# Causal mask by a selection after the exponential, 32-column merges with a copied block, two-step norms, row-wise transfers and a new step order in a delta-rule attention and mixture kernel

## The chip, the cores and the metric

One core of a Trainium2 chip runs the whole problem as one program. The metric is the device time of one execution in microseconds. Three runs of the kernel before gave 469.35, 471.07 and 987.01 us; the median, 471.07 us, is what a new time is compared with. The profile was taken on one more execution, which took 472.51 us.

## The reference, cut to what matters

Two layers follow each other. The first is a recurrence with a state per head (4 batches, 8 heads, 768 positions, head size 48); the second is a causal attention per expert (4 experts of width 64), whose two best experts per token are mixed with softmax weights.

```python
k_n = k / (np.linalg.norm(k, axis=-1, keepdims=True) + 1e-06)
for t in range(S):                       # state starts at zero
    y[:, :, t] = q[:, :, t] @ state
    v_old = state^T k_n[t]
    state = state + beta[t] * outer(k_n[t], v[t] - v_old)
x = y as (batch, 768, 384)
logits = x @ w_gate                      # the two largest of 4 are kept: w
for e in range(4):
    q, k, v = x @ wq[e], x @ wk[e], x @ wv[e]
    scores = 0.125 * q @ k^T
    scores = np.where(causal, -1e9, scores)
    a = softmax(scores)
    out += w[e] * (a @ v @ wo[e])
```

The lines above are shortened; `causal` is true above the diagonal.

## The kernel before, in words

**Tiling.** The recurrence is cut into chunks of 64 positions. Four chunks of all heads of two batches make a *unit*; there are 6 units (`n` = 0 to 5; 3 after each other for batches 0 and 1, 3 for batches 2 and 3), each with 4 chunks (`c`). The attention of a unit's 256 query positions goes by batch (`b`), pair of experts (`y`), and pairs of 128-key blocks (`kp`). A unit `n` has `s = n % 3` earlier units before it, so its scores run over `kp` = 0 to `s`; the pair with `kp == s` holds the diagonal.

**Within a chunk** the recurrence becomes a triangular system. `gram` (L219) multiplies the keys with themselves on TensorE. `st_in` (L255) turns the Gram blocks on VectorE so that each partition holds one 32x32 system. `solve_pre` (L267, steps 0 to 5) takes the diagonal, makes the norm of each key from a bit trick and three Newton steps for the square root (L277 to L279), the factor `aa` = beta / norm² (L285), its negative `nn` (L290, L293), and multiplies the system by it (L291 for unit 0 on VectorE, L294 for the other units on POOL). `solve_step` (L304, steps 1 to 32) eliminates: two TENSOR_TENSOR per step (L316 and L317), on POOL for units 1 to 5 and on VectorE (L319, L320) for unit 0; step 31 is an affine selection (L323), step 32 a product with `aa` (L329) and a copy (L330). `st_out` (L336) and `st_nat` (L332) turn the result back into `TG` (tile `tt`) and `TN` (tile `tn`). For units 1 to 5 `merge1` (L365) and `merge2` (L375) combine the two 32-halves of a chunk into a 64x64 inverse: `merge1` makes `-M` with products of 32 columns; `merge2` multiplies `TN` with two 32-column blocks at once, an identity that stands at index 0 of `lanes(n)` and the block of `merge1`, so that one 64-column product gives both the copied block and the new one, and ScalarE copies all 64 columns (L385). `clear` (L387) sets the block below to zero on POOL. Unit 0 is built in another way (`gram_up` L237, `diag` L339, `expand` L349): its Gram blocks are masked on VectorE (L244), 16-wide systems are solved, and products on TensorE expand them.

**The chain of states.** For each chunk: `ks`, `u`, `s`, `q`, `y` (L416 to L463) on TensorE with one ScalarE or VectorE step after each. Each chunk needs the state of the one before. `spread` (L464) moves rows of the output (`h3`, tile `h`) to other partitions of `xh` by six small transfers from SP's queue (L469), three for one half and then three for the other.

**The second layer.** `proj_qk` (L476) and `proj_v` (L501) accumulate nine products each: three pairs of high and low parts, and within each pair the three 128-row groups `r`. `max_list` (L544) forms scores with a mask added by two bf16 products (`identb`, `mbias`) per block and half, and takes maxima (L568). `score` (L598) forms the transposed scores from three products and a fourth that subtracts the maximum (`SEL`, `MR`), and for the diagonal pair adds the mask by two more bf16 products per block and half; ScalarE takes the exponential (L622, L624, L625) into `at`. `av` (L627) multiplies `at` with the values; `norm`, `fin_t`, `fin_o` finish and store.

**Matmul records.** All matmuls are issued by the helper `mm` (L115 and L116), so the profile shows them on L116 and they are told apart by their tiles (`pm__66` to `pm__69` are four rotating PSUM banks). A product with plain fp32 operands leaves two records, one with float32r operands or bf16 leaves one.

**The order.** Nothing is scheduled by a compiler: each engine's queue is in program order, and that order is the string `ORDER` (L36), a list of steps written out by hand or by a planner, which L728 runs one after the other. `sv3.7` is solve step 7 of unit 3; `+13` stands for 13 *filler* products of a zero tile (`zb`, 128x128 by 256, bf16, L125). 298 of these stand in the list, nearly all before the merges of unit 1 (`m1`, `m2`); one more is issued ahead of it. Step names: `gr` gram, `gu` gram_up, `gq` gram_q, `si` st_in, `so` st_out, `sn` st_nat, `m1`, `m2` the merges (`m13.0` is `merge1` of unit 3), `cl` clear, `vt` scale_v, `hx` spread, `pj`, `pv` the projections, `mx`, `mp`, `mr` the maxima, `sc` score, `nm` norm, `ft`, `fo` the end, `cb` small_consts, `kc` pick_rows, `w` weights, `lc`, `lg`, `lq` loads, `vs` ones, `gt` gates.

Of the kernel before, what the change touches and what calls it, by code (L numbers as in the profile page):

```python
# [21 lines left out]
ATB = 7  # L22
NP = 8
NT = CH * NP
# [12 lines left out]
+21 gr0.0 gr0.3 cb gr0.1 gr0.2 si0 gq0.1 pre0.0 gu2 w2 pre0.1 w3 pre0.2 pre0.3 pre0.4 pre0.5 +16 gu3 sv0.1 sv0.2 sv0.3  # L37
+4 gu1 sv0.4 w4 sv0.5 sv0.6 +34 gq0.3 sv0.7 sv0.8 sv0.9 lc0.1 vt0.1 sv0.10 sv0.11 sv0.12 lq1.1 sv0.13 sv0.14 +10 gu0
vt0.0 w0 sv0.16 +13 gq0.0 so0 +34 gr1.3 +6 gr1.2 w5 +10 gr1.1 gr1.0 sn0 dg1 dg0 lq1.2 kc0 si1 pre1.0 dg2 +27 ex1.0 +7
ex1.1 pre1.1 pre1.2 kc1 pre1.3 dg3 pre1.4 w1 kc3 w6 ex0.0 pre1.5 sv1.1 +12 ex2.0 sv1.2 sv1.3 sv1.4 ks0.0 gq0.2 ex0.1  # L40
ex1.2 +15 ex2.1 +2 ex0.2 ex3.0 sv1.5 sv1.6 sv1.7 sv1.8 +5 ex0.3 sv1.9 lq1.0 +7 u0.0 gq1.1 +1 s0.0 +5 ks0.1 y0.0 ex3.1
+7 ex3.2 lc0.2 ex1.3 sv1.10 q0.1 vs0 sv1.11 +3 u0.1 +5 s0.1 sv1.12 sv1.13 lc0.3 ex2.2 +7 ex2.3 vt0.2 ks0.2 ex3.3 kc2
lq1.3 y0.1 u0.2 sv1.14 sv1.15 vt0.3 sv1.16 sv1.17 sv1.18 lg2.1 +9 q0.2 s0.2 +6 ks0.3 hx0.1.0 lg2.3 y0.2 sv1.19 lg2.2
pj0.0.0 pj0.0.2 lg2.0 gq1.3 sv1.20 q0.3 u0.3 gr2.0 sv1.21 sv1.22 sv1.23 sv1.24 +1 y0.3 gq1.2 sv1.25 sv1.26 mx0.0.0.0
+9 mx0.1.0.0 lc1.0 sv1.27 vs1 sv1.28 pv0.0.0 hx0.3.0 gr2.1 s0.3 gq1.0 +1 pj0.1.2 q1.0 gr2.2 sv1.29 sv1.30 sv1.31
sv1.32 so1 vt1.0 ks1.0 lg3.0 sn1 gr2.3 pj0.1.0 pv0.1.1 si2 lq2.2 m11.0 m11.1 +2 m21.0 +2 m21.3 cl1 mx0.0.1.1 u1.0
pre2.0 m21.1 mp0.0 m21.2 s1.0 lc1.1 pre2.1 pre2.2 pv0.0.1 vt1.1 mr0.0 lc1.2 ks1.1 pre2.3 vt1.2 y1.0 pre2.4 vs2
sc0.0.1.0 pre2.5 sv2.1 mx0.1.1.1 u1.1 q1.1 +1 s1.1 pv0.1.0 ks1.2 sv2.2 lq2.1 lc1.3 sv2.3 vt1.3 sv2.4 mp0.1 y1.1 u1.2
sv2.5 sv2.6 mr0.1 sv2.7 sv2.8 sv2.9 sc0.0.0.0 lg3.1 sc0.1.0.0 sv2.10 gt0 lq2.0 q1.2 sv2.11 sv2.12 hx1.1.0 sv2.13
sv2.14 s1.2 av0.0.3 av0.0.1 av0.0.0 av0.0.2 sc0.1.1.0 lc2.0 vt2.0 ks1.3 lg3.3 y1.2 sv2.15 sv2.16 nm0.0 pj1.0.0 q1.3  # L50
u1.3 gq2.0 gr3.0 sv2.17 sv2.18 y1.3 sv2.19 ft0.0 pj1.0.2 gr3.3 s1.3 av0.1.0 sv2.20 mx1.0.0.0 av0.1.1 av0.1.2 av0.1.3
mx1.0.0.1 gq2.2 hx1.3.0 sv2.21 pj1.1.2 pj1.1.0 pv1.1.0 lq3.1 sv2.22 mx1.0.1.2 +1 mx1.0.1.3 pv1.0.0 gr3.1 ks2.0 mp1.0
sv2.23 lq3.0 lg3.2 gr3.2 sv2.24 gq3.0 sv2.25 sv2.26 sv2.27 mr1.0 sv2.28 fo0.0.1 sc1.0.0.0 sc1.0.1.1 q2.0 sv2.29 lg4.0
# [36 lines left out]
def tile_kernel(ctx, tc, kq, kv, beta, wqk, wvg, wo, consts, out):  # L90
# [34 lines left out]
    def filler():  # L125
        mm(PY0[:, 0, 256:512], ZB[:, 0:128], ZB, False)
# [62 lines left out]
    for x in DB:  # L189
        G.memset(x, 0.0)  # L190
# [608 lines left out]
```

## Time and profile before

| What | us |
|---|---|
| Median of three runs | 471.07 |
| The profiled execution itself | 472.51 |
| Its span, first to last instruction | 470.7 |
| PE busy in the span | 445.1 |
| VectorE / ScalarE / POOL busy | 283.6 / 210.0 / 229.4 |
| Fillers, 299 products, busy | 42.5 |

In the profile PE is the matmul side of TensorE and PEld its weight loads. Matmuls are pipelined: the duration of one record (some 0.2 us for a small one) says little about the pace, which is read from the starts of successive records in the timeline. The granted clock of TensorE was 0.967 of full speed on average.

### The profile page before, as it was taken

Reading aid. Unit: us, or ns where it says so; the run is one execution under the profiler, and the core shown is the slowest. Engines: PE = TensorE matmul, PEld = TensorE weight load, DVE = VectorE, ACT = ScalarE, POOL = GpSimd, SP = SyncE. Lnnn points to the kernel's source line nnn. Section 1 sums busy time; section 2 is a strip of 40 time slices with the busy share of each in tenths; the row PEclk is TensorE's granted clock in tenths of the full one; section 3 lists DMA queues with packets and bytes.
Section 4 is the critical chain, followed back from the end, with each engine's and each line's share of the span. In section 5 each row is a group of like instructions: output and inputs, shape, how many; then the busy total and the mean of one; then the engine's idle time right before and its main releaser. Section 6 shows DMA issues by size and latency. Waiting matters only on the chain.

```text
span 470.7 us, 24388 instructions
## 1 busy us (share of the span) xinstructions
PE 445.1 (95%) x11019; PEld 396.6 (84%) x11019; DVE 283.6 (60%) x636; ACT 210.0 (45%) x535; POOL 229.4 (49%) x392
## 2 busy tenths in 40 slices
PE   6898999899998999979999999999999999999997
PEld 4676887779887988878978998998999888888996
DVE  1799743249866495766976939556474745654312
ACT  2207411126554257334464464554555454635562
POOL 4314669852389847898078855589821010000000
PEclk9699999899999899988997999999999999999999
DMA  8610012302241221251131402013310110110002
GB/s 267 250 52 31 3 38 88 113 21 81 85 131 21 70 97 54 63 162 22 72 88 42 138 13 89 3 51 123 111 47 10 53 49 25 37 67 19 3 18 85
DMA packets 18967, 32.89 MB, mean 70 GB/s; under 512 B 2864, under 2 KB 8880, under 8 KB 18864
## 3 DMA queue, kind: packets, MB, share of 16 engines
q1 hardware_dynamic: 18864, 31.34, 21.1%
q8 instruction: 86, 1.41, 1.3%
q14 instruction: 17, 0.14, 0.1%
HBM read 24.25 MB, written 4.72 MB: 62 GB/s over the span
## 4 chain that ended last, share of the span: by engine, by line
PE 77%; DVE 7%; DMA 5%; SPq 4%; issue 3%; ACT 3%; POOL 1%; ACTq 0%; DVEq 0%
PE pm__67 L116 17%; PE pm__69 L116 15%; PE pm__68 L116 14%; PE pm__66 L116 14%; PE py L116 9%; PE xu L116 7%; SPq L469 4%; DMA xh<-h 3%; DMA qf<-in_kq_dram 2%; DMA kf<-in_kq_dram 1%; DVE B L320 1%; DVE tm L319 1%; ACT tt L232 1%; DVE rr L278 1%; ACT VS L347 1%
## 5 line engine op out<-in xcount | busy, mean ns | idle before, releaser
L317 POOL TENSOR_TENSOR B<-B,tm 128x30 f32<-128x30 f32 (+9 forms) x150 | 78.2, 521 | 11.8
L316 POOL TENSOR_TENSOR tm<-B 128x30 f32<-128x30 f32 (+9 forms) x150 | 75.2, 501 | 10.6
L148 POOL TENSOR_TENSOR kv<-kv,nt 128x384 f32<-128x384 f32 x24 | 19.9, 831 | 50.4 <-DMA kv<-in_kv_dram 38.4
L116 PE MATMUL py<-zb 128*128 128x256 bf16 x299 | 42.5, 292 | 1.3 <-DVE zb L121 1.1
L116 PEld LDWEIGHTS <-zb 128*128 128x128 bf16 x299 | 28.9, 104 | 8.0 <-DVE zb L121 1.1
L389 POOL MEMSET tt<- 32x1024 f32 x10 | 9.5, 946 | 34.9 <-PE pm__66 L116 13.2
L116 PE MATMUL py<-qf,sb 48*48 48x64 f32 x704 | 23.9, 218 | 1.0 <-DVE h L463 1.0
L116 PEld LDWEIGHTS py<-qf,sb 48*48 48x48 f32 x704 | 21.0, 120 | 3.2 <-DVE h L463 1.2
L568 DVE TENSOR_REDUCE mx<-pm__66 128x1 f32<-128x512 f32 (+3 forms) x28 | 18.1, 646 | 7.0 <-PE pm__67 L116 6.9
L429 ACT ACTIVATE ub<-xu 128x384 f32<-128x384 f32 x24 | 11.8, 493 | 22.0 <-PE xu L116 18.5
L462 DVE TENSOR_TENSOR xh<-py,xh 112x384 fp32r<-112x384 f32 x24 | 13.3, 556 | 13.0 <-ACT h L461 13.0
L460 ACT ACTIVATE xh<-py 112x384 fp32r<-112x384 f32 x24 | 11.8, 493 | 20.8 <-PE py L116 20.5
L260 DVE STREAM_TRANSPOSE B<-tt 32x1024 f32<-32x1024 f32 x10 | 19.8, 1978 | 0.2
L116 PE MATMUL xu<-xs,tt 64*64 64x48 f32 x768 | 17.9, 227 | 1.7 <-issue 1.4
L116 PE MATMUL pm__66<-xh,wqkh 128*128 128x256 f32 x96 | 16.9, 311 | 2.5 <-DMA xh<-h 2.3
L423 DVE TENSOR_TENSOR xs<-kv,xu 128x384 f32<-128x384 f32 x22 | 12.1, 548 | 11.7 <-PE xu L116 3.7
L568 DVE TENSOR_REDUCE mx<-pm__69 128x1 f32<-128x512 f32 (+3 forms) x24 | 14.9, 620 | 5.8 <-PE pm__66 L116 5.7
L116 PE MATMUL pm__69<-mbias,identb 64*128 64x128 bf16 x128 | 18.3, 225 | 0.0
L116 PEld LDWEIGHTS xu<-xs,tt 64*64 64x64 f32 x768 | 15.0, 142 | 3.8 <-issue 2.3
L116 PEld LDWEIGHTS pm__66<-xh,wqkh 128*128 128x128 f32 x96 | 14.4, 213 | 3.3 <-issue 2.8
L568 DVE TENSOR_REDUCE mx<-pm__67 128x1 f32<-128x512 f32 (+3 forms) x24 | 14.8, 616 | 2.9 <-PE pm__68 L116 2.9
L116 PE MATMUL pm__66<-mbias,identb 64*128 64x128 bf16 x114 | 16.4, 225 | 0.0
(358 smaller groups left out, 1610.4 us busy)
## 6 DMA issues: line engine op xcount, KB each, us to landing
kv<-in_kv_dram SPq DMA_DIRECT2D x24, 384.0 KB, 3.5
kf<-in_kq_dram SPq DMA_DIRECT2D x24, 256.0 KB, 3.7
qf<-in_kq_dram SPq DMA_DIRECT2D x24, 256.0 KB, 4.4
out_dram<-ot SPq DMA_DIRECT2D x24, 192.0 KB, 1.9
xh<-h SPq DMA_DIRECT2D x72, 32.0 KB, 2.1
wst<-in_wqk_dram SPq DMA_DIRECT2D x3, 256.0 KB, 5.5
csb<-in_consts_dram SPq DMA_DIRECT2D x1, 256.0 KB, 5.6
wst<-in_wvg_dram SPq DMA_DIRECT2D x1, 256.0 KB, 5.2
```

Of the source, the lines that this page charges most:

```text
L116: T.matmul(o, lhsT=a, rhs=b, start=start, stop=stop, skip_group_check=True)
L148: G.tensor_tensor(vt, vt, PR[n]["nt"][:, c * NP:c * NP + NP, None].to_broadcast([128, NP, HD]), op=OP.mult)
L260: V.transpose(B[r:r + 32], gf[r:r + 32, :, 0:32].rearrange("p t j -> p j t"))
L316: e.tensor_tensor(tv, bc(Z[:, i:i + 1, i + 1:]), bc(Z[:, 0:i, i:i + 1]), op=OP.mult)
L317: e.tensor_tensor(Z[:, 0:i, i + 1:], Z[:, 0:i, i + 1:], tv, op=OP.add)
L389: G.memset(TG[n % 2][r + 32:r + 64, :, 0:32], 0.0)
L423: V.tensor_tensor(eight(XB), eight(vt), PX, op=OP.subtract)
L429: S.activation(eight(UB), PX, AF.Copy)
L460: S.activation(hi, Y[:, :, 0:3], AF.Copy)
L462: V.tensor_tensor(lo, Y[:, :, 0:3], hi, op=OP.subtract)
L469: nc.sync.dma_start(xh[r + HD:r + 64, :, i].bitcast(F32), h3[r + 16 * i:r + 16 * i + 16].bitcast(F32))
L568: V.tensor_reduce(dst.rearrange("p (y x) -> p x y", x=2)[:, x, y:y + per], P[x], axis=AX.X, op=OP.max)
```

## The change

- The score mask: the two bf16 mask products per block and half disappear from `score`; after the exponential, POOL selects in `at` (two 128x128 blocks in one instruction), setting what lies beyond the diagonal to zero. The masks in the maxima stay; the table that they use holds one orientation only.
- `merge2` multiplies 32 columns only. The block that the identity product gave is copied by POOL in a new step `mv` (`move`), two copies of 32x256 per chunk; the identity blocks go from `small_consts`.
- `gram_up` masks by three ScalarE copies per bank with a scale per partition, in place of one VectorE product; the first 16 columns are set to zero once by POOL.
- `solve_pre` has five steps: another start constant, two Newton steps, the first with a factor, and `nn` made directly from the reciprocal.
- `spread` issues its six transfers by row group, both halves of a group after each other; `proj_qk` and `proj_v` go through their nine products by row group.
- The table of constants has 760 columns in place of 1076.
- 64 products of 32x32 by 16 columns (`MINI`) are issued before the list.
- A new `ORDER` for all steps: 276 fillers, 20 `mv` steps, no `pre*.5`.

```diff
@@ ORDER
-+21 gr0.0 gr0.3 cb gr0.1 gr0.2 si0 gq0.1 pre0.0 gu2 w2 pre0.1 w3 pre0.2 pre0.3 pre0.4 pre0.5 +16 gu3 sv0.1 sv0.2 sv0.3
...
++kc2 lc0.1 lq1.0 +42 gr0.0 +2 gr0.1 gr0.2 +1 gr0.3 si0 pre0.0 pre0.1 pre0.2 pre0.3 pre0.4 vt0.0 ks0.0 cb sv0.1 sv0.2
+sv0.3 sv0.4 kc3 sv0.5 sv0.6 sv0.7 w4 sv0.8 sv0.9 w1 sv0.10 vt0.1 sv0.11 w5 gu2 gu1 +71 gu0 sv0.12 sv0.13 sv0.14 +1
...
+lq1.1 hx0.3.0 lc1.1 sv1.29 sv1.30 pre2.0 sv1.31 sv1.32 +3 pj0.1.2 so1 sn1 pv0.0.0 vt1.1 vt1.0 mv1.0 pre2.1 pre2.2
+pj0.1.0 kc0 pre2.3 ks1.0 mv1.2 lg3.0 lq2.0 +1 m11.1 mv1.1 m11.0 mv1.3 lq2.1 cl1 +7 m21.2 +4 m21.0 gq1.1 mx0.1.1.1 u1.0
...
+    for _ in range(MINI):
+        mm(PY0[0:32, 0, 256:272], ZB[:, 0:32], ZB[:, 0:16], False)
...
+    for x in UP:
+        G.memset(x[:, :, 0:16], 0.0)
...
         for f in range(2):
-            V.tensor_tensor(o[:, 4 * f:4 * f + 4], g[f], bmask[:, None, :].to_broadcast([128, 4, 64]), op=OP.mult)
+            for k in range(1, 4):
+                S.activation(o[:, 4 * f:4 * f + 4, 16 * k:16 * k + 16], g[f][:, :, 16 * k:16 * k + 16], AF.Copy,
+                             scale=bmask[:, k:k + 1])
...
-        elif k < 4:
+        elif k < 3:
+
+            half = 0.5 * (1 - 3.043e-4 * (k == 1))
             V.reciprocal(r, g0)
-            V.scalar_tensor_tensor(r, r, 0.5, ss, op0=OP.mult, op1=OP.mult)
-            V.scalar_tensor_tensor(g0, g0, 0.5, r, op0=OP.mult, op1=OP.add)
-        elif k == 4:
+            V.scalar_tensor_tensor(r, r, half, ss, op0=OP.mult, op1=OP.mult)
+            V.scalar_tensor_tensor(g0, g0, half, r, op0=OP.mult, op1=OP.add)
+        elif k == 3:
...
+            V.scalar_tensor_tensor(nn, r, -1.0, bta[:, n], op0=OP.mult, op1=OP.mult)
+        else:
+            if n:
+                G.tensor_tensor(pr["B"], pr["B"], nn[:, None, :].to_broadcast([128, 32, 32]), op=OP.mult)
+            else:
+                Z = blocks(n)
+                V.tensor_tensor(Z, Z, by_col(nn), op=OP.mult)
             V.tensor_tensor(aa, r, bta[:, n], op=OP.mult)
...
+    def move(n, c):
+
+        o = TG[n % 2][:, NP * c:NP * c + NP]
+        for r, _ in HA:
+            G.tensor_copy(o[r:r + 32, :, 0:32], o[r:r + 32, :, 32:64])
+
     def merge2(n, c):
...
-        W = bank(128, NP, 64)
+        W = bank(128, NP, 32)
...
-                mm(W[r:r + 32, i].rearrange("p (a b) -> p a b", a=2), TN[r:r + 32, t], ws[r:r + 32, 0:t + 2:t + 1], True)
+                mm(W[r:r + 32, i], TN[r:r + 32, t], ws[r:r + 32, t + 1], True)
         for r, _ in HA:
-            S.activation(o[r:r + 32], W[r:r + 32], AF.Copy)
+            S.activation(o[r:r + 32, :, 32:64], W[r:r + 32], AF.Copy)
...
+    def spread(n, c):
+        xh, h3 = XH[n, c // 2]
+        for i in range(3):
+            for r, _ in HA:
+                nc.sync.dma_start(xh[r + HD:r + 64, :, i].bitcast(F32), h3[r + 16 * i:r + 16 * i + 16].bitcast(F32))
...
-        for a, b in ((wqkh, 0), (wqkh, 1), (wqkl, 0)):
-            for r in range(3):
+        for r in range(3):
+            for a, b in ((wqkh, 0), (wqkh, 1), (wqkl, 0)):
                 mm(P[:, y], a[:, r, w], xh[:, b, r], j == 0, j == 8)
...
             for r, x in HA:
-                mm(P[x][:, j, q0:], SEL[r:r + 64, 2 * y + x], MR[r:r + 64, n % 2, b, q0:], False, not dg)
-            for h in range(2 * dg):
-                for r, x in HA:
-                    mm(P[x][:, j, 128 * j:128 * j + 128], identb[r:r + 64, h], mbias[r:r + 64, 1, h], False, h == 1)
+                mm(P[x][:, j, q0:], SEL[r:r + 64, 2 * y + x], MR[r:r + 64, n % 2, b, q0:], False)
...
                 S.activation(A[x][:, 1, 128:], P[x][:, 1, 128:], AF.Exp, scale=0.125)
+                d = A[x].rearrange("p j (h q) -> p (j h) q", h=2)[:, ::3]
+                G.affine_select(d, d, pattern=[[0, 2], [1, 128]], compare_op=OP.is_ge, fill=0.0, base=0,
+                                channel_multiplier=-1)
```

More of the change, by code (lines that the diff above doesn't have):

```diff
@@ L23 @@
 NP = 8
+MINI = 64
 NT = CH * NP
@@ L36 @@
 ORDER = """
-+21 gr0.0 gr0.3 cb gr0.1 gr0.2 si0 gq0.1 pre0.0 gu2 w2 pre0.1 w3 pre0.2 pre0.3 pre0.4 pre0.5 +16 gu3 sv0.1 sv0.2 sv0.3
[L38 to L41, printed above, removed]
@@ L153, in tile_kernel @@
     KF = VS.rearrange("p a b c d -> p (a b c d)")
-    cst = cp.tile([128, 564], F32, name="cst")
+    cst = cp.tile([128, 504], F32, name="cst")
     bta = cp.tile([128, NU, 32], F32, name="bta")
-    csb = wk.tile([128, 512], F32, name="csb", tag="at", bufs=ATB)
+    csb = wk.tile([128, 2, 128], F32, name="csb", tag="at", bufs=ATB)
     load_k(0, 0)
@@ L164, in tile_kernel @@
     load_chain(0, 0)
-    nc.sync.dma_start(cst[:, 240:], consts[:, 752:1076])
-    nc.sync.dma_start(csb, consts[:, 240:752])
+    nc.sync.dma_start(cst[:, 240:], consts[:, 496:760])
+    nc.sync.dma_start(csb.rearrange("p h q -> p (h q)"), consts[:, 240:496])
     for c in range(CH):
@@ L172, in tile_kernel @@
     kmask = cst[:, 208:240]
-    bmask = cst[:, 500:564]
+    bmask = cst[:, 500:504]
     identb = cp.tile([128, 2, 128], BF16, name="identb")
-    mbias = cp.tile([128, 2, 2, 128], BF16, name="mbias")
+    mbias = cp.tile([128, 2, 128], BF16, name="mbias")
     TG = [cp.tile([128, NT, 64], F32, name=f"tt{i}") for i in range(2)]
@@ L507, in proj_v @@
         j = 0
-        for a, w in ((0, wvgh), (0, wvgl), (1, wvgh)):
-            for r in range(3):
+        for r in range(3):
+            for a, w in ((0, wvgh), (0, wvgl), (1, wvgh)):
                 mm(P, xh[:, a, r, b], w[:, r], j == 0, j == 8)
@@ L565, in one @@
                     for r, x in HA:
-                        mm(P[x][:, j, 128 * (nb - 1):], identb[r:r + 64, h], mbias[r:r + 64, 0, h], False, h == 1)
+                        mm(P[x][:, j, 128 * (nb - 1):], identb[r:r + 64, h], mbias[r:r + 64, h], False, h == 1)
             for _, x in HA:
@@ L696, in tile_kernel @@
             for kind, fn in (("lc", load_chain), ("vt", scale_v), ("lg", load_k), ("lq", load_q), ("gr", gram), ("gq", gram_q),
-                             ("ks", chain_ks), ("u", chain_u), ("q", chain_q), ("s", chain_s), ("y", chain_y), ("m2", merge2)):
+                             ("ks", chain_ks), ("u", chain_u), ("q", chain_q), ("s", chain_s), ("y", chain_y), ("mv", move), ("m2", merge2)):
                 step(kind, fn, n, c)
         for c in (1, 3):
-            step("hx", lambda n, c, _: (spread(n, c, 0), spread(n, c, 64)), n, c, 0)
+            step("hx", lambda n, c, _: spread(n, c), n, c, 0)
         for kind, fn in (("si", st_in), ("so", st_out), ("sn", st_nat), ("cl", clear), ("gt", gates)):
             step(kind, fn, n)
-        for k in range(6):
+        for k in range(5):
             step("pre", solve_pre, n, k)
```

127 lines of the change are left out of this document (55 added, 72 removed).

## The prediction

> **What bounds the kernel now.** I read the page first: busy shares, slices, and the chain that ended last.
>
> ```profile
> span 470.7 us, 24388 instructions
> PE 445.1 (95%) x11019; PEld 396.6 (84%) x11019; DVE 283.6 (60%) x636; ACT 210.0 (45%) x535; POOL 229.4 (49%) x392
> ...
> PE   6898999899998999979999999999999999999997
> ...
> POOL 4314669852389847898078855589821010000000
> PEclk9699999899999899988997999999999999999999
> ...
> PE 77%; DVE 7%; DMA 5%; SPq 4%; issue 3%; ACT 3%; POOL 1%; ACTq 0%; DVEq 0%
> ```
>
> TensorE is busy 445.1 of 470.7 us and carries 77% of the chain, so the time is TensorE's own queue plus its 25.6 us of holes. POOL's digits stop in slice 29: it solves for units 1 to 5 and is then free. Next I cut the span where the granted clock changes, and where POOL clears a unit's block (a clear stands between two units). Columns: length, then busy time and count of PE, PEld, DVE, ACT, POOL, then clock, DMA share, GB/s.
>
> ```profile
> 0.00:20.53 20.53, 13.88 (x374) 10.49 (x378) 8.11 (x20) 6.55 (x14) 8.65 (x15) 0.75 0.85 296
> ...
> 88.80:92.21 3.41, 3.41 (x19) 3.41 (x17) 0.69 (x1) 0.60 (x1) 2.94 (x7) 0.50 0.36 138
> ...
> 153.65:157.07 3.42, 3.42 (x19) 3.42 (x18) 0.00 (x0) 0.20 (x1) 2.98 (x6) 0.50 0.56 182
> ...
> 208.27:215.09 6.82, 6.49 (x97) 6.05 (x97) 2.77 (x8) 1.49 (x5) 5.96 (x12) 0.50 0.28 97
> ...
> 245.81:252.64 6.83, 6.83 (x131) 5.81 (x127) 3.92 (x10) 2.93 (x8) 6.13 (x12) 0.50 0.01 2
> ```
>
> ```profile
> 113.93:178.44 64.51, 62.24 (x1670) 55.68 (x1670) 46.50 (x101) 33.09 (x92) 42.51 (x72) 0.97 0.25 77
> 178.44:237.30 58.86, 55.45 (x1428) 50.08 (x1424) 40.07 (x89) 27.49 (x69) 41.24 (x70) 0.94 0.27 78
> ```
>
> After 20.5 us there are four stretches at half clock, 3.41 + 3.42 + 6.82 + 6.83 = 20.5 us, which cost up to half of that, 10.2 us. In a middle unit TensorE fills 62 of 64.5 and 55 of 59 us, POOL 41 to 42.5. So three things can move the time: TensorE instructions, holes with the slow clock behind them, and POOL if it loses its 17 to 22 us of room per unit.
>
> **The change part by part.** *Merge products, 64 to 32 columns.* The two merge steps of unit 2 stand side by side in the timeline: the first kind has 32 columns already, the second 64.
>
> ```profile
> 176.09 1.20 PE L116 MATMUL pm__67<-tt 32*32 32x32 f32 x64
> ...
> 179.19 1.08 PE L116 MATMUL pm__66<-B,tn 32*32 32x64 f32 x32
> ```
>
> Each fp32 product leaves two records, so one `m2` step is 32 records. They take 1.08 us now; at the pace of the row above, 1.20 / 64 x 32 = 0.60. That is 0.48 us less in each of 20 steps: **-9.6 us** on TensorE, at most -10.8 (the ends of the runs counted in the two rows overlap with what follows), at least -8. ScalarE's copy is halved with it, off the path. The Trainium skill, "TensorEngine Tiling (Array Packing)", section "Instruction Overhead", speaks against this: a matmul has about 60 cycles of overhead, so one with a free dimension of 1 lasts as long as one of 60, and a dimension that is already small should not be cut. By that rule 64 to 32 columns gives next to nothing and the sum would be 9 us worse. The two rows disagree with it: 18.8 ns a record against 33.8.
>
> *Score mask.* One diagonal score step, one of its two halves (the other has the same starts):
>
> ```profile
> 348.19 0.28 PE L116 MATMUL pm__69<-MR,SEL 64*128 64x256 f32 x1
> ...
> 348.31 0.23 PE L116 MATMUL pm__69<-mbias,identb 64*128 64x128 bf16 x1
> ...
> 348.38 0.22 PE L116 MATMUL pm__69<-mbias,identb 64*128 64x128 bf16 x1
> ...
> 348.41 0.30 PE L116 MATMUL pm__69<-QHI,KHI 64*128 64x128 f32 x1
> ...
> 348.89 0.23 PE L116 MATMUL pm__69<-mbias,identb 64*128 64x128 bf16 x1
> ...
> 349.11 1.20 PE L116 MATMUL pm__67<-tt 32*32 32x32 f32 x64
> ```
>
> Starts 348.31 to 348.41 and 348.89 to 349.11: 0.10 and 0.22 us, together 0.32 per step, some of the second a change of tile shape that stays. There are 6 units x 2 batches x 2 = 24 such steps: between 24 x 0.25 and 24 x 0.34, I take **-7 us**. The masks in the maxima stay.
>
> *What POOL gets for these.* 48 selections of 128x256 and 40 copies of 32x256.
>
> ```profile
> L323 POOL TENSOR_SCALAR_AFFINE_SELECT B<-B 128x1024 f32<-128x1024 f32 x5 | 6.3, 1267 | 0.4
> ...
> L346 POOL COPY VS<-tn 32x256 f32<-32x256 f32 x8 | 3.1, 390 | 0.4
> L317 POOL TENSOR_TENSOR B<-B,tm 128x30 f32<-128x30 f32 (+9 forms) x150 | 78.2, 521 | 11.8
> ```
>
> A selection lies between 0.32 us (a quarter of 1267 ns) and 0.52 (the mean solve step of the third row); the L346 row has its length of 256 elements, so I take 0.45 with the step between instructions. A copy: 0.39 + 0.08 = 0.47. A unit has 8 of each: 7.4 us more in 41 to 42.5, so 49 of a unit that lasts 61.7 now (mean of the two rows) and 57 if it gets a sixth of the sum below. What hides them is this room; without it they cost 7.4 us a unit. A selection also puts a wait into POOL's queue: behind it stand the solve steps of the next unit, and for those wait `so`, `sn`, both merges and then `u`. I count 0 here; the slower rival prices it. Before `av` it adds the selection's own length plus one solve step in front of it, about 1 us; in the new order `av` mostly stands several steps after its score, and a bank of other TensorE work lies between.
>
> *Norms, Gram masks, constants.* These are VectorE's in the first unit, where nothing else can run ahead:
>
> ```profile
> 18.48 0.41 DVE L244 TENSOR_TENSOR up<-pm__69,cst 128x256 f32<-128x256 f32 x1
> ...
> 21.38 0.35 DVE L277 RECIPROCAL rr<-g 128x32 f32<-128x32 f32 x1
> 21.77 0.19 DVE L278 SCALAR_TENSOR_TENSOR rr<-rr,ss 128x32 f32<-128x32 f32 x1
> 22.00 0.19 DVE L279 SCALAR_TENSOR_TENSOR g<-g,rr 128x32 f32<-128x32 f32 x1
> ...
> 23.75 0.74 DVE L290 TENSOR_SCALAR nn<-aa 128x32 f32<-128x32 f32 x1
> ...
> 37.65 1.97 DVE L337 STREAM_TRANSPOSE tt<-B 128x1024 f32<-128x1024 f32 x1
> ```
>
> ```profile
> 54.44 2.37 POOL L294 TENSOR_TENSOR B<-B,nn 128x1024 f32<-128x1024 f32 x1 [2.24 <-DVE nn L293]
> ...
> 99.76 0.24 POOL L330 COPY B<-aa 128x32 f32<-128x32 f32 x1
> ```
>
> Eight L244 products of 0.41 (3.3 us) go to ScalarE, a Newton step of 0.73 and the 0.74 of L290 go away: 4.8 us, and `so0` can start about that much before 37.65. In later units a Newton step goes away ahead of POOL's solve. None of this is TensorE time: it lets POOL's first solve (54.4 to 100 us) end earlier, and TensorE's queue, which holds fillers for that stretch, gets no shorter by it. ScalarE takes 24 short copies where it has little to do (6.55 of the first 20.53 us); the constants shrink by 316 columns x 128 x 4 bytes, 0.16 MB. I count 0, and -3 or +2 for the range.
>
> *Fillers and the 64 tiny products.* 298 fillers become 276:
>
> ```profile
> 1.13 4.88 PE L116 MATMUL py<-zb 128*128 128x256 bf16 x22 [1.13 <-DVE zb L121]
> ...
> 98.09 1.16 PE L116 MATMUL py<-zb 128*128 128x256 bf16 x9
> ```
>
> One filler costs 0.22 us at the start and (1.16 - 0.28) / 8 = 0.11 warm: -2.4 us. A tiny product lies between 19 ns (32x32, above) and a cold filler's 220, so 1.2 to 14 us for 64; by shape it is nearest the first, and I take 1.4 us: net **-1**. They run before the first Gram product, as do 21 more fillers; that one now starts at 5.94, but the fourth cannot end before 13.3, since TensorE stood still until 13.07 with nothing to wait for:
>
> ```profile
> 13.07 0.28 PE L116 MATMUL pm__66<-kf 48*32 48x32 f32 x5 [3.96 <-issue]
> ```
>
> So up to 4 us more at the start lie in that hole.
>
> *Transfers row by row, products row by row.* The wait on `xh`:
>
> ```profile
> 87.31 0.71 PE L116 MATMUL pm__69<-xh,wqkh 128*128 128x256 f32 x4 [1.87 <-DMA xh<-h]
> ...
> 153.18 1.09 PE L116 MATMUL pm__66<-xh,wqkh 128*128 128x256 f32 x5 [1.87 <-DMA xh<-h]
> ```
>
> ```profile
> 79.75 4.43 SPq L469 DMA_DIRECT2D xh<-h  x6
> ```
>
> Six issues pass SP one after the other and the last pair decides. Today the third of nine products needs it; afterwards six can go before it. That is four products, 4 x 0.12 = 0.5 us, for each of about three long waits: -1.5.
>
> *New order.* It moves every step, past every queue. By the text, the solve tokens stand earlier against the matmuls than before, and the fillers are again nearly all before the first unit's merges. Which holes survive cannot be read from a list. Of 25.6 us of holes and 10.2 us of slow clock I take -4.5 (beside the 1.5) and -5. The slow stretches follow the waits: 88.80 follows the 87.31 row, 153.65 the 153.18 row. The Trainium skill, "TensorE: Matmul & The Clock Gate", Part 1, has the clock fall after an idle window of about 3.4 us. By that rule holes of 1.9 us cost no clock, the -5 would be 0 and my time 447.5; the trace shows half clock behind just such holes.
>
> **Sum.** -9.6 - 7 - 1 - 1.5 - 4.5 - 5 = -28.6. The profiled execution took 472.5 us (span 470.7), so 443.9; it stands 1.4 above the median of 471.07, so I predict **442.5**.
>
> **The rivals.**
> *Only the work goes (chance 0.24).* The order brings as many holes as it removes: 9.6 + 7 + 1 = 17.6, time 453.5. For: a new order has new waits. Against: the longest holes are tied to single transfers.
> *More than that (0.13).* All four slow stretches and half of the holes vanish: 17.6 + 10.2 + 12.8 = 40.6, time 430.5.
> *The removed work was covered (0.08).* Waits on the state chain take its place, and only the fillers (1), the `xh` waits (1.5) and the 3 us of the start's bound count: 472.5 - 5.5 - 1.4 = 465.6, no change at 2% (9.4 us, about what a measurement of this kernel can tell). Against: TensorE fills 94 to 96% of a unit.
> *POOL becomes the bound (0.07, slower).* Per unit POOL then has 49 us, and between two solves `so`, `sn` (1.97 each) and the merges, some 6 us: 55, against 61.7 now. Four scores a unit make it wait for ScalarE's exponential; if each holds it w us, a unit takes 55 + 4w. From there on TensorE's savings count only behind the last solve, some 8 us of the 28.6. Slower is reached where five units lose those 8, 1.6 each: w = 2.1. At w = 3 a unit takes 67, +5.3 x 5 = 26.5: 472.5 + 26.5 - 8 - 1.4 = 489.6. For: POOL is strictly in order, as its rows show. Against: in the last third, with most of the large scores, it is free.
> The rule on small dimensions would give 452 by my sum. That is inside the first rival, and I give it 0.03 of that chance.
>
> **How the numbers follow.** The forecast has 0.48; its own range, from merge 8 to 10.8, mask 6 to 8, fillers and tiny products -1 to +7 (14 - 2.4, 4 of it in the hole at 13.07), holes and clock 5 to 17, is 434 to 459. The range is 428 to 463: it takes in the first two rivals, and leaves out covered work and POOL. Faster by over 2% (below 461.6): 0.48 + 0.24 + 0.13 less 0.02 = 0.83; within 2%: 0.10; slower: 0.07.
>
> **What would show it.** `B,tn` records at 32x32 with some 12 us busy instead of 22; 192 `mbias` records instead of 384; PE busy near 420; selections near 0.45 us; first clear well before 113.9; fewer stretches at 0.50. I am wrong if POOL shows long waits on exponentials with PE holes at the merges, or if PE's holes stay at 25 us.

## The result, and the profile after

The changed kernel takes 449.97 us, the median of four executions (447.6 to 451.46); the kernel before took 470.21 beside it (467.26, 469.35, 471.07 and one execution of 987.01). The ratio is 0.9585, 95% interval 0.951 to 0.966. Ratios leave out every execution over 1.5% above the fastest of its kernel (three of the four with all edits in the old order, below). The forecast was 442.5 with a range of 428 to 463: right in direction and inside its range, 7.5 us too low. The profiled execution took 449.0 us, its span 447.3, at a mean granted clock of 0.973 (0.967 before).

The page of the changed kernel, the lines that were read first of the kernel before:

```profile
span 447.3 us, 24245 instructions
...
PE 422.8 (95%) x10869; PEld 378.7 (85%) x10869; DVE 280.3 (63%) x610; ACT 203.5 (46%) x555; POOL 263.8 (59%) x484
...
POOL 5044789858888678698687787989873210000010
PEclk9679999999998996999999999999999999999999
...
PE 69%; DVE 12%; issue 2%; ACT 1%; DVEq 0%; ACTq 0%
...
L633 POOL TENSOR_SCALAR_AFFINE_SELECT at<-at 128x256 f32<-128x256 f32 x48 | 19.1, 408 | 90.5 <-ACT at L631 74.8
...
L388 POOL COPY tt<-tt 32x256 f32<-32x256 f32 x40 | 15.7, 392 | 10.6 <-DVE tt L346 9.0
```

TensorE is busy for 22.3 us less (445.1 to 422.8), but its holes have hardly moved: span less busy is 24.5 us, 25.6 before. POOL carries 34.4 us more and spends 74.8 us waiting for exponentials, without TensorE waiting for POOL: the waits of the matmul side of the changed kernel (in total, times, longest):

```profile
PE py L118 <- ACT py L415: 5.6, 1, 5.6
PE pm__69 L118 <- issue: 4.1, 3, 3.6
PE pm__68 L118 <- DVE mx L578: 1.7, 1, 1.7
PE py L118 <- DVE h L474: 1.6, 1, 1.6
PE pm__69 L118 <- DVE KLO L506: 1.5, 1, 1.5
...
PE pm__67 L118 <- POOL VS L355: 0.2, 1, 0.2
```

No `xh` line is left, where the kernel before has these (longest 1.9 us) among its first rows:

```profile
PE pm__66 L116 <- issue: 4.4, 2, 4.0
PE pm__69 L116 <- DMA xh<-h: 2.4, 3, 1.9
PE pm__67 L116 <- DMA qf<-in_kq_dram: 2.3, 2, 1.6
PE pm__66 L116 <- DMA xh<-h: 2.3, 3, 1.9
```

The two longest waits of the changed kernel stand in the first 25 us, and its half-clock stretches are there too (columns as in the prediction):

```profile
16.97 0.28 PE L118 MATMUL pm__69<-kf 48*32 48x32 f32 x4 [3.61 <-issue]
...
24.85 0.37 PE L118 MATMUL py<-zb 128*128 128x256 bf16 x1 [5.61 <-ACT py L415]
```

```profile
14.51:28.17 13.66, 5.59 (x96) 4.43 (x96) 9.94 (x31) 4.42 (x12) 2.19 (x3) 0.50 0.40 145
140.81:144.22 3.41, 3.41 (x40) 3.21 (x36) 2.99 (x2) 1.84 (x7) 2.94 (x7) 0.50 0.19 40
168.11:174.94 6.83, 5.94 (x155) 4.73 (x158) 4.64 (x10) 1.24 (x3) 5.75 (x16) 0.50 0.03 5
```

Half clock after the start went from 20.5 to 10.2 us. The removed work shows in the timeline. First a merge of the second kind (`m2`), 1.08 us before; then, on VectorE, the turn of the first unit's Gram blocks (`si0`, called the first inversion below) and the hand-over of its solve (`so0`):

```profile
164.86 0.67 PE L118 MATMUL pm__67<-B,tn 32*32 32x32 f32 x32
```

```profile
17.89 1.93 DVE L266 STREAM_TRANSPOSE B<-tt 128x1024 f32<-128x1024 f32 x1
...
36.04 2.00 DVE L346 STREAM_TRANSPOSE tt<-B 128x1024 f32<-128x1024 f32 x1
```

VectorE's chain in the first unit is 18.15 us long here; before it ran from 14.38 to 37.65, 23.3 us. It starts 3.5 us later and its hand-over still comes 1.6 us earlier.

A ledger over the whole span, in us, adds up the distances from the start of each product to the start of the next, by kind (waits and half clock are in them):

| Products | before | after | change |
|---|---|---|---|
| merges of the second kind | 21.9 | 12.8 | -9.1 |
| score mask | 8.3 | 0 | -8.3 |
| scores and value products | 95.8 | 94.4 | -1.4 |
| projections (`pj`, `pv`) | 95.0 | 83.5 | -11.5 |
| fillers, tiny products | 42.9 | 40.8 | -2.1 |
| Gram products of the keys, with the start's holes | 23.4 | 31.8 | +8.4 |
| all else | 178.4 | 179.0 | +0.6 |

The removed work came out as forecast, the projections gave more, and the start took 8 us back. Two explanations are tested below. Theory: all of this is TensorE's work, and the edits pay wherever they stand. Rival: the edits pay only in an order of steps that leaves POOL's queue free at the right places, and the order is part of the gain.

### The profile page after: what moved, and what is told of

Its sections match the earlier page's. It is cut to its first block, busy times and chain, and to the rows that moved or that the text cites. A ratio compares the mean times of both kernels' runs of the same rounds, so it can differ in the third digit from the quotient of the medians.

```text
span 447.3 us, 24245 instructions
## 1 busy us (share of the span) xinstructions
PE 422.8 (95%) x10869; PEld 378.7 (85%) x10869; DVE 280.3 (63%) x610; ACT 203.5 (46%) x555; POOL 263.8 (59%) x484
## 4 chain that ended last, share of the span: by engine, by line
PE 69%; DVE 12%; issue 2%; ACT 1%; DVEq 0%; ACTq 0%
PE pm__68 L118 14%; PE pm__66 L118 13%; PE pm__69 L118 13%; PE pm__67 L118 12%; PE py L118 8%; PE xu L118 7%; DVE B L269 2%; DVE mx L578 1%; DVE B L266 1%; DVE tt L346 1%; DVE tn L343 1%; DVE KLO L506 1%; DVE rs L654 1%; DVE ss L282 1%; PE pm__69 L665 0%
## 5 line engine op out<-in xcount | busy, mean ns | idle before, releaser
L325 POOL TENSOR_TENSOR tm<-B 128x30 f32<-128x30 f32 (+9 forms) x150 | 74.3, 496 | 10.1
L633 POOL TENSOR_SCALAR_AFFINE_SELECT at<-at 128x256 f32<-128x256 f32 x48 | 19.1, 408 | 90.5 <-ACT at L631 74.8
L118 PE MATMUL py<-zb 128*128 128x256 bf16 (+1 forms) x341 | 42.0, 272 | 8.3 <-ACT py L415 5.6
L118 PEld LDWEIGHTS <-zb 128*128 128x128 bf16 (+1 forms) x341 | 28.9, 104 | 13.7 <-issue 6.2
L153 POOL TENSOR_TENSOR kv<-kv,nt 128x384 f32<-128x384 f32 x24 | 19.8, 832 | 25.6 <-DVE nt L294 16.0
L578 DVE TENSOR_REDUCE mx<-pm__67 128x1 f32<-128x512 f32 (+3 forms) x27 | 17.0, 630 | 9.6 <-PE pm__68 L118 5.6
L388 POOL COPY tt<-tt 32x256 f32<-32x256 f32 x40 | 15.7, 392 | 10.6 <-DVE tt L346 9.0
L452 DVE TENSOR_TENSOR sb<-sb,xu 112x384 f32<-112x384 f32 x20 | 11.0, 549 | 16.0 <-PE xu L118 12.2
L118 PE MATMUL pm__69<-xh,wqkh 128*128 128x256 f32 x108 | 20.8, 292 | 0.0
L578 DVE TENSOR_REDUCE mx<-pm__69 128x1 f32<-128x512 f32 (+3 forms) x21 | 12.6, 601 | 8.6 <-PE pm__66 L118 5.6
L578 DVE TENSOR_REDUCE mx<-pm__66 128x1 f32<-128x512 f32 (+3 forms) x25 | 15.7, 626 | 3.7 <-PE pm__67 L118 3.5
L118 PEld LDWEIGHTS pm__69<-xh,wqkh 128*128 128x128 f32 x108 | 17.2, 196 | 0.5 <-ACT os L647 0.2
L118 PE MATMUL pm__69<-QHI,KHI 64*128 64x256 f32 (+1 forms) x56 | 16.5, 295 | 0.0
```

Source lines behind the costliest of these rows:

```text
L118: T.matmul(o, lhsT=a, rhs=b, start=start, stop=stop, skip_group_check=True)
L153: G.tensor_tensor(vt, vt, PR[n]["nt"][:, c * NP:c * NP + NP, None].to_broadcast([128, NP, HD]), op=OP.mult)
L325: e.tensor_tensor(tv, bc(Z[:, i:i + 1, i + 1:]), bc(Z[:, 0:i, i:i + 1]), op=OP.mult)
L388: G.tensor_copy(o[r:r + 32, :, 0:32], o[r:r + 32, :, 32:64])
L452: V.tensor_tensor(eight(new), eight(state(n, c)), SP, op=OP.add)
L578: V.tensor_reduce(dst.rearrange("p (y x) -> p x y", x=2)[:, x, y:y + per], P[x], axis=AX.X, op=OP.max)
```

## The experiments

The times of the kernel before, run beside each group, are 468.07, 467.49, 467.90 and 466.33 us. One estimate is used throughout: span times mean granted clock stands for the span at full clock. It takes off half of every stretch at half clock, as if TensorE alone set the time there, so it is a lower bound. Its median is 456 us for the kernel before and 437 for the changed one.

**One edit at a time, in the old order.** Merge products of 32 columns, the copy by POOL at the head of the same step:

```diff
-        W = bank(128, NP, 64)
+        for r, _ in HA:
+            G.tensor_copy(o[r:r + 32, :, 0:32], o[r:r + 32, :, 32:64])
+        W = bank(128, NP, 32)
...
-                mm(W[r:r + 32, i].rearrange("p (a b) -> p a b", a=2), TN[r:r + 32, t], ws[r:r + 32, 0:t + 2:t + 1], True)
+                mm(W[r:r + 32, i], TN[r:r + 32, t], ws[r:r + 32, t + 1], True)
...
```

> The kernel before with 32-column products in merge2 and the copy of the block by POOL at the head of the same step, nothing else. Work theory (the time is TensorE's queue): -9.1 us, the difference of the merge records between the two traces, so about 461. Cover rival (the merges stand where the end waits for something else, or POOL's 40 copies hold the solve): no change, 468 to 472.

Measured: 475.38 us, ratio 1.016 (1.007 to 1.026), slower than either explanation expected. Its merge products do take 14.6 us instead of 21.9. TensorE's busy time falls only from 445.1 to 442.2, and its holes grow from 25.6 to 30.0 us. One long stretch at half clock, worth up to 8.5 us, stands against the gain:

```profile
179.42:196.49 17.07, 17.07 (x352) 14.21 (x354) 8.12 (x18) 4.28 (x11) 15.09 (x30) 0.50 0.10 30
```

No hole over 0.6 us stands just ahead of this stretch, so what brought it stays open. At full clock the runs stand at 453.5, 2.5 less than before; the clock (0.953 to 0.966 in its executions, 0.966 to 0.984 for the kernel before) turns that into a loss. The theory that the work pays wherever it stands has failed its first test.

Selection in place of the mask products:

```diff
-            for h in range(2 * dg):
-                for r, x in HA:
-                    mm(P[x][:, j, 128 * j:128 * j + 128], identb[r:r + 64, h], mbias[r:r + 64, 1, h], False, h == 1)
...
+                d = A[x].rearrange("p j (h q) -> p (j h) q", h=2)[:, ::3]
+                G.affine_select(d, d, pattern=[[0, 2], [1, 128]], compare_op=OP.is_ge, fill=0.0, base=0,
+                                channel_multiplier=-1)
```

> The kernel before with the mask of the scores by POOL's selection after the exponential and without the 192 mask products, old order. Work theory: -7 to -8 us, about 462.5, with POOL's idle room taking the 48 selections of 0.41 us. Rival (POOL in order): the old order was not laid out for selections, solve steps queue behind them while they wait for exponentials, holes before the merges of units 2 and 3 eat the gain: 468 to 480.

Measured: 497.21 us, ratio 1.065 (1.056 to 1.074), beyond the 480 that the rival went up to. Four views follow: waits of the matmul side; POOL's queue at the longest of them; the exponential and the value product that waits for POOL there; and another place in POOL's queue:

```profile
PE pm__66 L116 <- POOL at L624: 4.5, 1, 4.5
...
PE pm__67 L116 <- POOL at L624: 3.5, 1, 3.5
PE pm__68 L116 <- DVE lg L513: 3.5, 1, 3.5
```

```profile
138.32 0.56 POOL L317 TENSOR_TENSOR B<-B,tm 128x198 f32<-128x198 f32 x1
138.84 1.48 POOL L624 TENSOR_SCALAR_AFFINE_SELECT at<-at 128x256 f32<-128x256 f32 x4
```

```profile
133.90 0.30 ACT L622 ACTIVATE at<-pm__68 128x128 f32<-128x128 f32 x1
...
139.66 0.92 PE L116 MATMUL pm__66<-VS,at 128*64 128x65 f32 x12 [4.51 <-POOL at L624]
```

```profile
284.94 0.85 POOL L624 TENSOR_SCALAR_AFFINE_SELECT at<-at 128x256 f32<-128x256 f32 x2 [8.17 <-PE xu L116]
285.75 0.61 POOL L316 TENSOR_TENSOR tm<-B 128x240 f32<-128x240 f32 x1
```

The last exponential ends at 134.20, yet the selections start at 138.84: the solve steps that stand ahead of them in POOL's queue run first, and the value products wait at 139.66. That is the rival of the prediction (POOL in strict order) at both of its ends: at 284.94 POOL has stood for 8.17 us at a selection whose exponential was not there, with solve steps behind it. Such waits with a solve step behind them add up to 32 us in this kernel (5.25, 0.51, 4.51, 4.70, 8.17, 3.97, 2.12 and 2.95) and to 9 us in the changed one (the longest 2.98; one more, of 6.33 us, has copies of the merge behind it).

TensorE meets this delay a second time, by way of VectorE. The solve ends late, VectorE stands at its hand-over, and what is behind that in VectorE's queue comes late too. The third row below is the stretch at half clock that begins there:

```profile
242.90 1.94 DVE L337 STREAM_TRANSPOSE tt<-B 128x1024 f32<-128x1024 f32 x1 [4.45 <-POOL B L330]
...
244.98 0.42 PE L116 MATMUL pm__68<-tt 32*32 32x32 f32 x9 [3.48 <-DVE lg L513]
```

```profile
245.02:268.91 23.89, 23.89 (x456) 20.02 (x460) 11.94 (x30) 8.27 (x16) 16.62 (x29) 0.50 0.15 44
```

VectorE waits like this three times (12.1 us in all, never in the kernel before or the changed one), and TensorE's holes behind these waits are 2.69, 3.48 and 3.02 us. The holes that wait for POOL directly are 8 us. Together these come to 17 us; all holes grow by 18 (25.6 to 43.9). The half clock is the larger part: 58 us of it after the start, a clock of 0.93; at full clock the runs stand at 462, only 6 above before.

The selection in units 4 and 5 alone, when POOL has no solve left:

```diff
+            for h in range(2 * dg if n < 4 else 0):
...
+                if n < 4:
+                    continue
+                d = A[x].rearrange("p j (h q) -> p (j h) q", h=2)[:, ::3]
...
```

> The kernel before with the selection in units 4 and 5 only, whose scores come when POOL has no solve left; units 0 to 3 keep the mask products. Theory, what cost 29 us in the old order was POOL's queue (selections and solve steps of the next unit stuck behind each other): here nothing is behind them, 16 of 48 selections replace 128 of 384 products, a third of 7 to 8 us: -2.5, ratio 0.993 to 0.997, no PE hole on POOL. Rival, the selection itself costs (its own 0.4 us and the semaphores between exponential and product): then units 4 and 5 lose a third of 29 us, ratio 1.01 to 1.02.

Measured: 467.67 us, ratio 0.9992 (0.9949 to 1.0036). POOL still waits long, but nothing is behind it and no product waits for it:

```profile
POOL at L629 <- ACT at L625: 81.1, 7, 21.0
```

The loss is gone, and a cost of the selection itself (1.01 or more) is excluded. The expected gain (0.993 to 0.997) is not shown: the interval holds its smaller half and no gain at all. So the loss comes with the selections that have solve steps around them in the queue, not with the instruction.

Transfers and products row by row, as in the change's diff:

> The kernel before with the six transfers and the nine products by row group, nothing else. Prediction: -1.5 us (the last pair still has to land). Rival, from the trace after, where no wait for these transfers is left: the rows are what removed them, -5 us of waits and two half-clock stretches of 3.4 us (1.7 each): about -8, 462.

Measured: 465.48 us, ratio 0.9953 (0.9912 to 0.9994), 2.6 less than the 468.07 beside it, with an interval of 0.3 to 4.1: the -1.5 of the prediction lies in it, the rival's -8 does not.

**All edits in the old order** (the changed code with the list of before; the copy's step right ahead of its merge):

> The changed kernel with the order of before (the copy step set just ahead of each merge2, the norm steps renumbered), so every edit but the new order. Work theory: the merges and the mask, -17, and some of the rows: 450 to 454, and the new order gives 0 to 4 us. Rival (the order is what pays; without it POOL's new work opens waits): 460 or more, and the new order gives 10 or more.

Measured: 476.99 to 490.89 us in four executions, median 486.56; the lowest, 477, is taken as the bound from below, and the rival (460 or more) holds. POOL makes the value products wait as with the selection alone:

```profile
PE pm__66 L68 <- POOL at L583: 4.0, 1, 4.0
PE pm__67 L68 <- POOL at L583: 3.4, 1, 3.4
```

**The new order alone** (the code of before with the new list, without the copy's steps):

> The kernel before with only the order changed (the steps of the move are dropped from the list, the norm's steps are counted on by one; products, masks, transfers and norms as before). It completes the square: before 468, edits in the old order 486.6, all of it 450. Theory now: the edits' work (m2 9.1, mask 8.3, xh waits some 5 of the ledger) is real only where the order leaves TensorE no new wait; so the order alone gives 450 + 9 + 8 + 5 = 472, between 464 and 478, PE busy near 440 us and at least 20 us of holes. Rival: the order itself is the gain and the edits are nearly free under it: 450 to 458.

Measured: 475.6 us, ratio 1.022 (1.013 to 1.031). So neither half pays: edits alone 477 or more, order alone 475.6, together 450. The order alone also answers a question of the ledger: this kernel has the transfers and products of before and no wait on `xh` either (its `pj` and `pv` take 82.5 us in the ledger, 83.5 in the changed kernel). So where the new list puts the transfers is enough for the projections' 11.5 us. In the run with the rows alone they take 88.6 us, against 95.0 in the kernel before; the rows and the list win the same time, not one on top of the other. The longest waits of the order alone are others, and which of them the edits take away was not tested:

```profile
PE pm__67 L67 <- issue: 7.0, 4, 4.1
PE py L67 <- DVE h L414: 6.5, 2, 4.9
PE py L67 <- ACT py L352: 3.3, 1, 3.3
```

**Taking one edit out of the changed kernel.** The mask products back, no selection; then the 64 columns and the identity blocks back, no copy:

```diff
+            for h in range(2 * (kp == s)):
+                for r, x in HA:
+                    mm(P[x][:, j, 128 * j:128 * j + 128], mbias[r:r + 64, h], identb[r:r + 64, h], False, h == 1)
...
-                d = A[x].rearrange("p j (h q) -> p (j h) q", h=2)[:, ::3]
-                G.affine_select(d, d, pattern=[[0, 2], [1, 128]], compare_op=OP.is_ge, fill=0.0, base=0,
-                                channel_multiplier=-1)
```

> The changed kernel with the score mask as products again and no selections, all else as changed, the order too. Theory, work on TensorE: the 192 products come back at some 43 ns each, +8.3 us: 458, between 455 and 461, POOL busy 19 us less. Rival, the selections' wait in POOL's queue costs under the new order too: then what comes back on TensorE is paid by POOL's room, 447 to 452.

```diff
-        W = bank(128, NP, 32)
+        W = bank(128, NP, 64)
...
-                mm(W[r:r + 32, i], TN[r:r + 32, t], ws[r:r + 32, t + 1], True)
+                mm(W[r:r + 32, i].rearrange("p (a b) -> p a b", a=2), TN[r:r + 32, t], ws[r:r + 32, 0:t + 2:t + 1], True)
...
```

> The changed kernel with merge products of 64 columns again, the identity block put back and no copies on POOL. Theory, work on TensorE: the m2 records take 21.9 us again instead of 12.8, 450 + 9 = 459, between 456 and 462. Rival, they lie beside a wait: 448 to 453.

Measured: 459.71 us for the first (ratio 0.985, 0.976 to 0.994; 9.7 above 450, 12 by the ratios) and 457.16 for the second (0.978, 0.969 to 0.987; 7.2 above, 9 by the ratios). By the intervals of the ratios each of these differences is uncertain by some 5 us. The products themselves are back: in the ledgers of these runs the mask products take 6.4 us, and the merges 20.4 in place of 12.8. At full clock the two runs stand at 443 and 443 against 437. Within this uncertainty each edit is worth its own products in the new order, as the prediction's sum had it.

**POOL's room in the new order.** Each selection twice:

```diff
+                G.affine_select(d, d, pattern=[[0, 2], [1, 128]], compare_op=OP.is_ge, fill=0.0, base=0,
+                                channel_multiplier=-1)
```

> The changed kernel with each of the 48 selections issued twice (the second changes nothing). POOL gets 48 x 0.41 = 19.6 us more, 38 of it in the units whose solve it still has ahead shared by 4 a unit. Theory, POOL has room in the new order: 450 to 453, POOL busy near 283. Rival, POOL is already the bound beside TensorE: +1.6 us or more for each of units 1 to 5, 458 and above, with PE waits on POOL at the merges.

Measured: 447.26 us (447.1 to 449.99), ratio 0.961 (0.955 to 0.966), the time of the changed kernel. POOL is busy for 281.6 us, 17.8 more:

```profile
PE 423.4 (94%) x10869; PEld 379.9 (85%) x10869; DVE 278.0 (62%) x610; ACT 203.3 (45%) x555; POOL 281.6 (63%) x532
```

The prediction's "I count 0" for POOL holds in the new order, with as much again to spare; in the old order the same selections make the kernel 29 us slower, although they take products off TensorE.

**The start.** The 5.6-us hole is a wait for `cb`: ScalarE stands at the first scaled values (`ks0.0` needs `vt0.0`) with the constants' step behind it, and that step zeroes a region of the bank that the fillers write to. `cb` moved ahead of the first inversion:

```diff
-... +1 gr0.3 si0 pre0.0 ... pre0.4 vt0.0 ks0.0 cb sv0.1
+... +1 gr0.3 cb si0 pre0.0 ... pre0.4 vt0.0 ks0.0 sv0.1
```

> The changed kernel with the constants' step (cb) moved ahead of the first inversion, so that ScalarE does it before it waits for the first scaled values. Theory, the 5.6-us hole at 24.9 holds TensorE's own queue: it is gone, the fillers behind it start by 20, the first unit's Gram products of unit 1 come 3 to 5 us earlier and the whole is 445 to 448. Rival, the first solve on VectorE sets the start and TensorE only waits elsewhere: 449 to 451.

Measured: 451.89 us, ratio 0.965 (0.958 to 0.972): no gain. The hole has moved to the first expansion, which needs the first solve:

```profile
42.66 0.44 PE L118 MATMUL pm__67<-VS 64*64 64x64 f32 x2 [5.19 <-POOL VS L355]
```

And the solve has become longer, 16.79 to 38.39 us. VectorE's and POOL's rows of that kernel, side by side, show why:

```profile
28.11 0.25 DVE L329 TENSOR_TENSOR B<-B,tm 128x88 f32<-128x88 f32 x1
...
32.04 0.25 DVE L328 TENSOR_TENSOR tm<-B 128x88 f32<-128x88 f32 x1
32.09 1.35 POOL L220 TENSOR_TENSOR wqkl<-wst,wqkh 128x512 fp32r<-128x512 f32 x1 [4.13 <-ACT wqkh L219]
...
32.32 1.23 DVE L329 TENSOR_TENSOR B<-B,tm 128x88 f32<-128x88 f32 x1
```

An addition of the same size (L329) takes 0.25 us while POOL stands still and 1.23 beside one of POOL's subtractions of the weights' low parts. `cb` early let ScalarE prepare the weights earlier, and POOL's part of it fell onto the solve: 10 of the solve's 30 two-input instructions overlap a two-input instruction of POOL there, 5 in the changed kernel. The changed kernel pays for this too: the 28 instructions of its elimination steps take 9.7 us, against 6.8 in the kernel before and 13.1 here. The Trainium skill, "SBUF — State Buffer", section "Who interferes with whom", says that a VectorE instruction with two SBUF inputs contends with a GpSimd instruction that reads SBUF; the 0.25 against 1.23 us agree with it.

`cb` early and 21 fillers ahead of the first Gram product instead of 42:

> As the run before it, and 21 fillers ahead of the first Gram product instead of 42. Theory, the start's chain (fourth Gram product, first inversion, its solve) sets when everything else begins: the fourth Gram product ends near 12.4 to 14.5 instead of 17.5 (as in the run with the changed code in the old order), the first solve is handed on 3 to 5 us earlier than 36.0, and the time is 441 to 446. Rival, instruction fetch sets the pace of the first 400 records, whatever stands in them: the fourth Gram product still waits until 16 to 17, 446 to 450.

Measured: 448.49 us (ratio 0.959, 0.950 to 0.968), within the spread of the changed kernel. Its profiled execution was one of 1280 us and isn't read. The next run has the same start: there the fourth Gram product ends at 12.0 us and the hole comes behind it, at 16.20, so the rival's reason (the fourth product still waits until 16 to 17) does not hold, although its time does.

On top of that, all weights behind the first unit's diagonal blocks:

```diff
-... sv0.7 w4 sv0.8 sv0.9 w1 sv0.10 vt0.1 sv0.11 w5 gu2 ... gr1.1 w0 w2 +4 gr1.0 w3 w6 gr1.3 ... dg3 pre1.2
+... sv0.7 sv0.8 sv0.9 sv0.10 vt0.1 sv0.11 gu2 ... gr1.1 +4 gr1.0 gr1.3 ... dg3 w4 w1 w5 w0 w2 w3 w6 pre1.2
```

> As the run with cb early and 21 fillers, and all seven weight steps moved behind the first unit's diagonal blocks, so that POOL's subtractions of the weights' low parts no longer run beside VectorE's first solve. In the run with cb early the solve's additions took 1.2 us instead of 0.25 just while POOL subtracted (24.0 to 28.1 and 32.3 to 36.6), and the solve was handed on at 38.4 instead of 36.0. Theory, this overlap and not TensorE holds the start: no addition over 0.5 us beside a weight subtraction, first inversion to hand-over 15.5 to 16.5 us (18.2 in the changed kernel, 21.6 with cb early), hand-over by 32, POOL's first solve 3 to 6 us before 52.6, time 442 to 447. Rival, what follows TensorE's and POOL's queue takes it up again: hand-over early, time 448 to 452.

Measured: 448.22 us (446.0 to 459.94), ratio 0.9589 (0.954 to 0.964). The first half of the theory holds, the second does not:

```profile
12.54 1.90 DVE L266 STREAM_TRANSPOSE B<-tt 128x1024 f32<-128x1024 f32 x1
...
28.35 1.99 DVE L346 STREAM_TRANSPOSE tt<-B 128x1024 f32<-128x1024 f32 x1
```

```profile
52.56 0.72 POOL L220 TENSOR_TENSOR wol<-wst,woh 128x256 fp32r<-128x256 f32 x1
53.24 2.35 POOL L299 TENSOR_TENSOR B<-B,nn 128x1024 f32<-128x1024 f32 x1
```

```profile
151.89:175.78 23.89, 23.89 (x500) 19.71 (x500) 15.71 (x32) 7.75 (x21) 14.63 (x31) 0.50 0.15 47
```

The hand-over comes 7.7 us earlier than in the changed kernel (15.8 us after the inversion, no addition slowed), but POOL now subtracts the weights right ahead of its first solve, which starts at 53.24 instead of 52.60; and in the profiled execution a stretch of 23.9 us at half clock took up to 12 back. The weight steps take POOL 7.8 us there, from 45.7 on; the two rows of POOL show that a shorter start needs another place for them. No version here is better than the changed kernel by more than the spread.

## Why the prediction was right, and where it was wrong

*Merges, -9.6*: -9.1 in the ledger, 7.2 when taken out. The pace read from the two neighbouring merges was the right row. The rule of the Trainium skill that spoke against it ("TensorEngine Tiling (Array Packing)", section "Instruction Overhead") would have given next to nothing. The 640 records of this merge take 12.8 us with 32 columns and 20.4 with 64 in the same order of steps, so the rule fails here.

*Score mask, -7*: -8.3 in the ledger; 9.7 when taken out, where the products themselves are 6.4. Right within what the runs can tell.

*POOL, "I count 0"*: right for this kernel (the doubled selections cost nothing), but not for the reason given. Room per unit was not what decided: in the old order POOL has the same room and loses 29 us. The rival on POOL (chance 0.07) had the right mechanism for the old order, with one half missing: it counted POOL waiting at a selection, while the prediction put "one solve step in front of it, about 1 us" before `av`. In the old order it is several steps, 138.84 against 134.20 us. In the new list no value product waits for POOL, and POOL's own waits ahead of solve steps are 9 us in place of 32.

*`xh`, -1.5 by rows*: the edit alone gave 2.6. All of these waits went, and the order alone is enough for that: 2.4 and 2.3 us in the two rows above, none after.

*Start*: VectorE's chain was shortened by 5.1 us against 4.8 worked out, and gave TensorE nothing, as counted. That the two numbers agree is partly luck: the new order also moved 2.4 us of `gq` products (L253) out of this chain, and POOL's subtractions lengthened the solve by 2.9 us. The hole at 13.07 was to hide up to 4 us of the work added ahead of the Gram products. It hid none: it now stands at 16.97, 128 records further on, 3.61 us long, and VectorE's chain starts 3.5 us later.

*Slow clock, -5*: after the start half clock fell by 10.3 us, worth up to 5. The start itself lost 1.7 of that (13.7 instead of 10.2 us at half clock).

*The step that failed is "other holes, -4.5"*: beside the `xh` waits, which went, the holes grew by some 4 us. I had said that they cannot be read from a list, and took a gain all the same. That left 24.5 us, and "PE's holes stay at 25 us" was one of the prediction's own signs of being wrong; the other signs it named came as it wanted (first clear at 105.19 us, PE busy 422.8, selections 0.41). One hole could be read: `cb` had moved behind `ks0.0`, so ScalarE must wait for the first scaled values before it zeroes the bank of the fillers. That hole alone is 5.6 us. The sum of -28.6 came out as -23.5 between the two profiled executions; the other 2.4 of the 7.5 us come from the step to the medians, 1.4 taken off and 1.0 to be added. That the sum is so near is in part luck: the 11.5 us off the projections and the 8.4 us more at the start, neither of them in the sum at this size, nearly cancel. Removing that hole did not win the 5 us either, since the first solve is late at the next place.

What stays open: why half clock lasts 3.4 us after one hole and up to 23.9 after another. In the run with the selection alone the two longest stretches are 37.5 of the 58 us. It is also open why the new list loses without the edits.

## What to carry to other kernels

Before moving an operation to an engine with room, look at which instructions stand ahead of the moved one in that engine's queue when its input is ready, and which behind it while it is not: the total of free time decides neither. In this kernel removed work was worth its own length only after the order of the steps had been made anew around it; test an edit and its order as a pair, since each alone can lose what both win. A hole on TensorE of 2 us is to be priced with the half clock that may follow it.

## What the runs showed of the hardware beside that

*Half clock mostly follows holes of about 2 us.* Counted over thirteen profiles (all but that of the 1280-us execution), after the first 40 us and for holes that begin at full clock: with a hole of over 2.3 us half clock began in the hole or within 4 us of its end in 14 of 15 cases, from 1.8 to 2.3 us in 6 of 7, from 1.4 to 1.8 in 11 of 32, from 0.5 to 1.4 in 9 of 66. Not every stretch has such a hole: of 43 stretches 8 have none over 1 us ahead of them, among them that of 17.07 us above and the one at 245.81 us of the kernel before. The stretches last a multiple of 3.41 us, mostly one or two. The Trainium skill, "TensorE: Matmul & The Clock Gate", Part 1, names an idle window of about 3.4 us. In these profiles half clock mostly followed holes well below it, from 1.8 us on.

*A hole at a fixed count of instructions at the start.* With no releaser named, TensorE's hole at the start stands behind its record 222 or 223 (the kernel before and the four with one edit, at 13.07 to 13.63 us; the new order alone, at 15.08) or behind record 350 (the changed kernel and the five made from it with a readable trace, at 15.94 to 17.57): the places go by the count of instructions and lie 128 products with their 128 weight loads apart. Each of these holes is 3.3 to 5.0 us long. Two smaller ones fit the same places: 1.4 us behind record 223 with all edits in the old order, and 2.7 us behind record 350 with the new order alone. The Trainium skill, "Runtime: NRT & Kernel Launch", section "Instruction fetch mechanics", gives fetched blocks of 256 instructions, which agrees with that distance, and calls the cost of a block's end mostly hidden, which these holes are not. That TensorE waits for instructions there is inferred from the count; no row names it.
